# Attention scores in 32-row by 64-column tiles of the TensorE array, in a two-layer transformer kernel

## The chip, the cores and the metric

The kernel runs on one core of a Trainium2 chip. The metric is the device time of one execution in microseconds; a result is the median of several runs. A core has five engines with an instruction stream each: TensorE (PE, matmuls and their weight loads), VectorE (DVE), ScalarE (ACT, activations), GpSimd (POOL) and SyncE (SP, which issues DMAs). An engine takes its instructions in order, and the streams meet at semaphores.

## What is computed

Two layers, each a sliding-window attention and an MLP, on one sequence of 2048 tokens of width 576 (32 heads of 18, window 256, MLP width 4608). Cut to what matters here:

```python
def attention(x):                       # x is layer-normalized
    q, k, v = split(x @ wqkv)           # 32 heads of 18
    scores = einsum("qd,kd->qk", q, k) * 18 ** -0.5
    mask = (q_idx - k_idx >= 0) & (q_idx - k_idx < 256)
    p = softmax(where(mask, scores, -1e9))
    return (p @ v) @ wo

for layer in range(2):                  # the same weights in both
    x = x + attention(layernorm(x))
    x = x + gelu(layernorm(x) @ w1 + b1) @ w2 + b2
```

## The kernel before, in words

**Tiling.** The 2048 tokens are 16 blocks of 128. A chunk `k` is four blocks (512 tokens) of one layer; there are eight chunks, four a layer (`CH`, L455). The 32 heads are eight groups `g` of four heads. The q and k of a group lie transposed in `qT` and `kT`, head `j` of the group in partitions 32j to 32j+31 (18 used, the rest zero), so that the four heads of a group can be four row tiles of the TensorE array, 32 rows by 128 columns each.

**A score unit** (`scores`, L777). Keys of block `so` (counted from the chunk's first block, so -1 and -2 are the blocks before it) are seen by the queries of blocks `so`, `so+1` and `so+2`: the first of these is the diagonal block, the last the far end of the window. The twelve (key block, query block) pairs of a chunk and group are packed into three units of 512 columns by `units_of` (L765). A part of a unit is `(so, qo, nq, col)`: key block, first query block, number of query blocks, first column in PSUM. For each part, and for each of the four heads, one matmul (L789) multiplies the 128 keys (stationary) by up to 384 queries (moving). Scores come out transposed, keys in partitions and queries in columns, one head a PSUM bank: a unit takes four of the eight banks, in two pairs out of 0-1, 2-3, 4-5 (`SC`). In a layer's first chunk the parts with keys before the sequence fall away, and two of its three units shrink to 384 and 256 columns.

ScalarE then takes Exp of two banks at a time into `pT` (L798), GpSimd zeroes what the mask excludes in the diagonal and far blocks (`affine_select`, L819), and TensorE multiplies by v (`pv`, L834) with tiles of 128 rows by 32 columns, four heads beside each other in one PSUM bank (`OUT`). VectorE transposes that bank (L845), divides by the row sums (L848, L851) and transposes again for the output projection (`two_out`, L699, also used for q, k and v).

**MLP.** `G_part` (L899) computes a third of the MLP's first layer for a chunk (the 64 left-over rows at L919 in 64-row tiles, the four full blocks at L931), with Gelu on ScalarE (L934). `mm2` (L946) multiplies by the second weight (L960) into a bank out of `FILL`, and VectorE adds it to the residual (L880). ScalarE loads a table at each change between Exp and Gelu (L973).

**What sets the order.** Nothing runs in the order it is written. Each step is a task with a cost, a latency, a priority and the tiles that it reads and writes; `Plan.schedule` (L257) simulates the five engines, takes the task that can start first (ties by priority), gives PSUM banks out of a list of choices (`Bank`, `place`, L266), adds `SWITCH` (0.095) to TensorE's cost when the tile mode changes (`mode`: "r" scores, "c" P·V, "h" the 64-row tiles, "f" full), and writes the order down as each engine's fixed instruction stream. Score units and MLP groups share a first-in-first-out list ("pa"). `PL.nudge` (L463) adds a number to the priority of every task of a named stage; "ea2" is the first part of the attention of chunk 2, "mb3" the second third of `mm2` of chunk 3, "q5.1" the projections of its second block, and so on.

**Start.** VectorE clears PSUM banks 7 to 4 (L599 to L601, priority -7), then takes the statistics of the first blocks (L620, priority -6), normalizes (L643), and TensorE transposes (L657) into a bank of `FILL`; ScalarE copies out (L660).

Of the kernel before, what the change touches and what calls it, by code (L numbers as in the profile page):

```python
# [421 lines left out]
def build_kernel(nc, A_x, A_wqkv, A_wo, B_x, B_w1, B_b1, B_w2, B_b2, out):  # L422
# [36 lines left out]
    PL = Plan(S, 8)  # L459
# [3 lines left out]
    PL.nudge = {"b": 29.4, "ea0": -2.66, "ld0": 0.01, "ld0+": -29.79, "eb0": 0.53, "ec0": 3.31, "le0+": 114.63, "q1.0": -118.82, "q1.1":  # L463
                -98.11, "q1.2": -0.91, "q1.3": -7.44, "t0": -5.22, "ea1": -89.48, "ga0": -171.5, "ga0+": 5.04, "eb1": -15.16, "ma0": 12.04,
                "ma0+": -17.91, "gb0": -145.98, "ec1": -2.99, "le1+": 16.44, "le1": -20.83, "mb0": -3.03, "q2.1": 45.54, "q2.2": 88.61,
                "q2.3": 55.86, "t1": -120.53, "gc0": -19.84, "gc0+": -25.1, "ln3": 57.08, "mc0": 4.28, "mc0+": 148.11, "ga1": -4.06, "ga1+":
                -6.33, "eb2": -3.01, "ma1": 5.64, "ma1+": 13.09, "gb1": -0.44, "ec2": 3.21, "mb1": 7.94, "mb1+": -24.34, "q3.0": 14.13,
                "q3.1": 131.09, "q3.2": 4.89, "q3.3": 1.84, "t2": -15.58, "gc1": 7.36, "gc1+": -31.57, "mc1": 17.31, "mc1+": -1.81, "ga2":
                -27.48, "ga2+": 158.23, "eb3": 36.01, "ma2": 50.85, "ma2+": 24.11, "gb2": 23.88, "gb2+": 71.77, "ec3": -0.31, "mb2": 60.21,
                "mb2+": -145.98, "q4.0": 0.58, "q4.1": 63.81, "q4.2": 55.53, "t3": 61.03, "gc2": 154.1, "gc2+": 8.93, "ln5": 14.44, "ea4":  # L470
                19.04, "mc2": 63.19, "ga3": 18.64, "ga3+": 0.44, "eb4": 14.59, "ma3": 30.2, "ma3+": 0.16, "gb3": -9.23, "gb3+": -6.16,
                "mb3": 45.14, "q5.0": 113.74, "q5.1": 29.89, "q5.2": -8.93, "q5.3": 76.56, "t4": -2.66, "gc3": 88.61, "gc3+": -48.97, "ln6":
                -15.57, "ea5": -72.82, "mc3": -2.47, "mc3+": 76.5, "ga4+": -33.16, "eb5": 2.91, "ma4": 29, "ma4+": 17.98, "gb4": -4.52,
                "gb4+": -7.43, "mb4": 59.81, "mb4+": -8.12, "q6.0": 1.38, "q6.1": 19.98, "q6.2": -18.44, "q6.3": 63.81, "gc4": 92.87,
                "gc4+": 84.52, "ln7": 31.11, "ea6": -2.66, "mc4": 24.73, "mc4+": 0.51, "ga5": 11.4, "ga5+": 1.49, "eb6": -0.34, "ma5":
                52.45, "ma5+": -6.49, "gb5": -32.33, "gb5+": 51.26, "ec6": -3.2, "mb5": 0.24, "mb5+": -3.62, "q7.0": 24.18, "q7.2": 137.8,
                "q7.3": 1.6, "t6": -24.34, "gc5": 5.59, "gc5+": -171.5, "ea7": 41.87, "mc5": 136.49, "mc5+": -1.6, "ga6": -32.64, "eb7":
                31.31, "ma6": 44.85, "ma6+": -1.66, "gb6": 0.02, "gb6+": -4.59, "ec7": -0.12, "mb6": 104.87, "mb6+": 63.38, "t7": -16.91,
                "gc6+": -0.75, "mc6": -119.39, "mc6+": -8.02, "ga7": -61.44, "ga7+": -11.43, "ma7": -14.13, "ma7+": 9.77, "gb7": 1, "mb7":
                3.96, "mb7+": -8.3, "gc7": 53.28, "mc7": 65.68, "": 0.88}  # L480
# [40 lines left out]
    FILL = (7, 6, 5, 4)  # L521
    OUT = (7, 6, 5, 4)
# [3 lines left out]
    def two(b):  # L526
        return ps[:, b.no * 512:(b.no + 2) * 512].rearrange("p (j c) -> p j c", j=2)
# [71 lines left out]
    for i in OUT:  # L599
        b = Bank((i,))  # L600
        add("dve", lambda e, b=b: e.memset(bank(b), 0.0), writes=[b], cost=0.56, lat=0.1, prio=-7, alloc=[b])  # L601
# [36 lines left out]
    def ln_norm_T(t, i, dst, dname, prio, src=None, srcres=None, dup=False, pe=False):  # L638
# [12 lines left out]
        if pe:  # L651
            b = Bank(FILL)

            def fn(e):
                ins = None
                for c in range(KD):
                    ins = e.transpose(bank(b).bitcast(BF16)[:, c * 128:(c + 1) * 128], xn[:, sl, c * 128:(c + 1) * 128], ident[:, :])  # L657
                return ins
            add("pe", fn, reads=rd + ["ident"], writes=[b], cost=0.5, prio=prio, alloc=[b])
            add("act", lambda e: e.copy(dst[:, :, i * 128:(i + 1) * 128], bank(b).bitcast(BF16)[:, 0:KD * 128].rearrange("p (c q) -> p c q", c=KD)),  # L660
                reads=[b], writes=[f"{dname}{i}"], cost=0.6, lat=0.17, prio=prio)
            return
# [55 lines left out]
    def qkv(k, i, prio0):  # L718
        l, t0, nt = CH[k]
        A = l * NT + t0 + i  # L720
        for n, w in enumerate("qkv"):
# [10 lines left out]
            else:  # L732
# [16 lines left out]
                if k == 0 and (w == "k"):  # L749
                    b = Bank(FILL)  # L750
# [26 lines left out]
    def scores(k, g, parts, prio):  # L777
        l, t0, nt = CH[k]
        T0 = l * NT + t0
        qs, qname = q_of(k)  # L780
# [3 lines left out]

        def fn(e):
            ins = None
            for (so, qo, nq, col) in parts:
                for j in range(4):
                    ins = e.matmul(two(bs[j // 2])[:, j % 2, col:col + nq * 128], k_of(T0 + so)[0][32 * j:32 * j + 32, g, :],  # L789
                                   qs[32 * j:32 * j + 32, g, qo * 128:(qo + nq) * 128], start=True, stop=True, tile_position=(32 * j, 0))  # L790
            return ins
        rd = [f"{qname}{qo + i}" for (so, qo, nq, col) in parts for i in range(nq)] + [k_of(T0 + p[0])[1] for p in parts]
        ncol = sum(p[2] for p in parts) * 128
# [205 lines left out]
    bb = Bank(FILL)  # L999
# [32 lines left out]
    for k in range(NK + 1):  # L1032
        b = 4 * k
# [112 lines left out]
```

## Time and profile before

| | |
|---|---|
| three runs, median (all) | 894.95 us (894.55, 894.95, 897.05) |
| the profiled execution | 897.23 us, of it 895.5 us of span |
| granted TensorE clock, mean | 0.998 |
| score matmuls (L789) | 1408, each with a weight load |
| Exp (L798) | 384, 345.8 us busy |
| masks (L819) | 368, 283.5 us busy |
| P·V matmuls (L834) | 1408 |
| L960, L931, L699 qkv, L919 matmuls, busy | 309.5, 255.0, 136.0, 39.7 us |

The busy rows of a page give the time in which an engine had an instruction in work, the share of the span and the number of instructions. TensorE's matmuls overlap, since one starts while the one before it drains; so the durations of single matmuls don't add up, and the distance from one start to the next is the price. Weight loads (PEld) run beside the matmuls.

### The profile page before, as it was taken

What the parts mean: (1) busy time and instruction counts of PE and PEld (TensorE: products, weight loads), DVE (VectorE), ACT (ScalarE), POOL (GpSimd) and SP (SyncE); (2) the same over time, 40 slices, a digit from 0 to 9 for tenths busy, and PEclk for the clock granted to TensorE, in tenths of its full rate; (3) what the DMA queues carried; (4) which work ended last, traced back from release to release, by engine and by line L of the source; (5) the groups of instructions that cost most, each with busy time, mean ns of one, the idle gap of its engine ahead of it and who ended that gap; (6) DMA issues with size and microseconds to landing.
All of it is one profiled execution on the core that took longest, in us unless ns stands there. A gap on an engine that the chain in (4) does not pass through costs nothing.

```text
span 895.5 us, 19577 instructions
## 1 busy us (share of the span) xinstructions
PE 864.4 (97%) x7849; PEld 506.5 (57%) x7901; DVE 410.1 (46%) x969; ACT 615.8 (69%) x737; POOL 366.2 (41%) x504
## 2 busy tenths in 40 slices
PE   5898999999999999999999999999999999999998
PEld 4555455656566565665655655556556545556665
DVE  6789223863357351763427633375134523161111
ACT  3976888577767788366773868747777689844443
POOL 3677544274244662224431544416444266231100
PEclk9999999999999999999999999999999999999999
DMA  6788537742477333853457342682537632446431
GB/s 177 139 172 173 179 119 182 178 109 81 149 166 158 120 120 98 183 124 121 130 119 181 71 158 86 143 198 67 165 119 147 184 125 71 144 126 176 153 96 50
DMA packets 182649, 122.25 MB, mean 137 GB/s; under 512 B 107424, under 2 KB 181024, under 8 KB 182560
## 3 DMA queue, kind: packets, MB, share of 16 engines
q1 hardware_dynamic: 179152, 115.47, 49.5%
q0 software_dynamic: 1584, 3.54, 1.5%
q10 hardware_dynamic: 1824, 1.99, 0.7%
q8 instruction: 63, 1.03, 0.5%
q14 instruction: 26, 0.21, 0.1%
HBM read 91.28 MB, written 2.36 MB: 105 GB/s over the span
## 4 chain that ended last, share of the span: by engine, by line
PE 54%; DVE 1%; issue 1%; DMA 1%; ACT 1%; POOL 0%
PE ps L960 21%; PE ps L931 18%; PE ps L699 6%; PE ps L789 3%; PE ps L919 3%; PE ps L834 3%; ACT pT L798 1%; DVE x_res L880 0%; DMA xnTa<-xn 0%; DVE st_all L620 0%; DMA xnTm<-xn 0%; DVE xn L643 0%; DVE xn L648 0%; POOL rstd L633 0%; DVE xn L883 0%
## 5 line engine op out<-in xcount | busy, mean ns | idle before, releaser
L819 POOL TENSOR_SCALAR_AFFINE_SELECT pT<-pT 128x512 bf16<-128x512 bf16 (+1 forms) x368 | 283.5, 794 | 266.6 <-ACT pT L798 262.0
L798 ACT ACTIVATE pT<-ps 128x1024 bf16<-128x1024 f32 (+2 forms) x384 | 345.8, 972 | 58.3 <-PE ps L789 57.8
L934 ACT ACTIVATE hT<-ps,b1col 128x512 bf16<-128x512 f32 x288 | 197.8, 687 | 192.8 <-PE ps L931 188.3
L960 PE MATMUL ps<-w_sb,hT 128*128 128x288 bf16 x2304 | 309.5, 287 | 0.2
L960 PEld LDWEIGHTS ps<-w_sb,hT 128*128 128x128 bf16 x2304 | 213.9, 98 | 81.9 <-issue 24.9
L931 PE MATMUL ps<-xnTm,w_sb 128*128 128x512 bf16 x1100 | 255.0, 380 | 4.9 <-issue 3.2
L931 PEld LDWEIGHTS ps<-xnTm,w_sb 128*128 128x128 bf16 x1152 | 109.6, 98 | 137.0 <-issue 19.1
L880 DVE TENSOR_TENSOR x_res<-ps,x_res 128x288 f32<-128x288 f32 x216 | 95.9, 448 | 169.0 <-PE ps L960 158.4
L699 PE MATMUL ps<-wqkv,xnTa 128*128 128x288 bf16 x960 | 136.0, 289 | 3.5 <-DVE qn L742 1.9
L845 DVE STREAM_TRANSPOSE oq<-ps 128x512 f32<-128x512 f32 x64 | 45.8, 715 | 179.0 <-PE ps L834 178.8
L699 PEld LDWEIGHTS ps<-wqkv,xnTa 128*128 128x128 bf16 x960 | 88.4, 98 | 41.4 <-issue 7.8
L742 DVE CAST qn<-ps 128x288 bf16<-128x288 f32 x120 | 53.2, 449 | 35.1 <-PE ps L699 33.0
L942 POOL TENSOR_TENSOR x_res<-x_res,b2bc 128x576 f32<-128x576 f32 x32 | 40.8, 1274 | 69.2 <-ACT hT L934 69.2
L789 PE MATMUL ps<-qT,kT 32*128 32x384 bf16 (+2 forms) x1216 | 64.1, 276 | 2.2 <-ACT pT L798 2.0
L631 POOL TENSOR_SCALAR vtmp<-mv_all 128x1 f32<-128x1 f32 (+1 forms) x43 | 8.5, 197 | 121.4 <-DVE mv_all L622 120.6
L834 PE MATMUL ps<-pT,vA 128*20 128x384 bf16 (+2 forms) x1408 | 50.7, 276 | 2.0 <-ACT pT L798 0.9
L620 DVE BATCH_NORM_STATS2 st_all<-x_res 128x6 f32<-128x288 f32 x104 | 44.8, 448 | 1.2
L919 PE MATMUL ps<-xnTm,w_sb 64*128 64x512 bf16 x288 | 39.7, 381 | 5.5 <-ACT pT L798 3.3
L789 PEld LDWEIGHTS ps<-qT,kT 32*128 32x128 bf16 x1216 | 19.5, 92 | 44.1 <-issue 25.1
L699 PE MATMUL ps<-wo_sb,attT 128*128 128x288 bf16 x320 | 42.8, 286 | 0.1
L834 PEld LDWEIGHTS ps<-pT,vA 128*20 128x20 bf16 x1408 | 25.7, 90 | 26.8 <-issue 13.4
L729 DVE CAST vA<-ps 128x288 bf16<-128x288 f32 x64 | 28.8, 454 | 23.7 <-PE ps L699 23.4
(47 smaller groups left out, 347.6 us busy)
## 6 DMA issues: line engine op xcount, KB each, us to landing
w_sb<-in_B_w_dram SPq DMA_DIRECT2D x48, 864.0 KB, 5.4
w_sb<-in_B_w_dram SPq DMA_DIRECT2D x48, 768.0 KB, 4.7
w_sb<-in_B_w_dram SPq DMA_DIRECT2D x96, 48.0 KB, 4.4
x_res<-in_A_x_dram POOLq DMA_DIRECT2D x3, 1152.0 KB, 7.0
out_dram<-xn SPq DMA_DIRECT2D x16, 144.0 KB, 1.8
wqkv<-in_A_wqkv_dram ACTq DMA_DIRECT2D x3, 576.0 KB, 6.9
w_sb<-in_A_x_dram SPq DMA_DIRECT2D x2, 576.0 KB, 4.2
wo_sb<-in_A_wo_dram SPq DMA_DIRECT2D x4, 144.0 KB, 2.6
```

The source lines that it names most:

```text
L699: ins = e.matmul(bank(bs[o])[:, 0:HB], lhs(c), rhs(c, o * HB), start=(c == 0), stop=(c == KD - 1))
L742: add("dve", lambda e, b=bs[o], dst=dst: e.tensor_copy(dst, heads_of(bank(b))), reads=[bs[o]], writes=[f"qn{sl}h{o}"], cost=0.375, lat=0.1 ...
L789: ins = e.matmul(two(bs[j // 2])[:, j % 2, col:col + nq * 128], k_of(T0 + so)[0][32 * j:32 * j + 32, g, :], qs[32 * j:32 * j + 32, g, qo * ...
L798: add("act", lambda e, h2=h2: e.activation(pT[:, sl, 2 * h2:2 * h2 + 2, lo:hi], two(bs[h2])[:, :, lo:hi], ACT.Exp, scale=SCALE), reads=[bs ...
L819: add("pool", lambda e, ap=ap, pat=pat, sgn=sgn, kind=kind: e.affine_select(ap, ap, pattern=pat, compare_op=(ALU.is_ge if kind == "d" else ...
L834: ins = e.matmul(bank(bo)[32 * j:32 * j + VW, qo * 128:(qo + nq) * 128], vA[:, (T0 + so) % VS, 8 * j + g, :], pT[:, sl, j, col:col + nq * ...
L845: add("dve", lambda e: e.transpose(oq[:, 0:4 * nt, :].rearrange("p b c -> p (b c)"), bank(bo)[:, 0:nt * 128]), reads=[bo, f"aq{(g - 1) % G ...
L880: add("dve", lambda e: e.tensor_tensor(x_res[:, t, sl], bank(b)[:, 0:HB], x_old[:, t, sl], ALU.add), reads=[b] + ([f"xin{t}"] if first els ...
L919: ins = e.matmul(bank(bk)[:, 0:n], w1_sb[64 * b:64 * b + 64, sl, col:col + 128], xnTm[64 * b:64 * b + 64, k % 2, 4, 0:n], start=True, stop ...
L931: ins = e.matmul(bank(bk)[:, 0:n], w1_sb[:, sl, col:col + 128], xnTm[:, k % 2, c, 0:n], start=False, stop=(c == 3))
L934: add("act", lambda e, ff=ff, fl=fl, bk=bk: e.activation(hT[:, fl, 0:n], bank(bk)[:, 0:n], ACT.Gelu_apprx_tanh, bias=b1col[:, ff:ff + 1]), ...
L960: ins = e.matmul(bank(b)[:, 0:HB], hT[:, fl, i * 128:(i + 1) * 128], w2_sb[:, fl, hh * HB:(hh + 1) * HB], start=(fl == 0), stop=(fl == NFH ...
```

## The change

The score matmul of 128 keys is split in two by keys: the lower 64 keys go to the tile at columns 0 to 63 of the array (PSUM partitions 0 to 63), the upper 64 to columns 64 to 127. Each half takes only the queries that some of its keys can see: on the diagonal block the upper half leaves out the first 64 queries, on the far block the lower half leaves out the last 64. So 64 x 64 corners of the PSUM tile are no longer written; Exp still reads them, and the mask zeroes them. All eight banks are therefore cleared at the start, and the steps that put bf16 transposes into PSUM at the beginning (the first normalized blocks, the first k, b1) use banks 7 and 6 alone, which scores never use. `OUT`, the banks of P·V, shrinks to (7, 6) too. The planner's cost of a score unit follows the columns of the larger half. Exp, the masks and P·V are as before. All values of `PL.nudge` are new.

```diff
-    PL.nudge = {"b": 29.4, "ea0": -2.66, "ld0": 0.01, "ld0+": -29.79, "eb0": 0.53, "ec0": 3.31, "le0+": 114.63, "q1.0": -118.82, "q1.1":
...
+    PL.nudge = {"b": -0.69, "ea0": -0.47, "ld0": 1.9, "ld0+": -0.51, "eb0": 38.45, "ec0": -25.47, "le0+": -6.05, "q1.0": -0.95, "q1.1":
...
-    OUT = (7, 6, 5, 4)
+    OUT = (7, 6)
...
-    for i in OUT:
+    for i in range(8):
         b = Bank((i,))
         add("dve", lambda e, b=b: e.memset(bank(b), 0.0), writes=[b], cost=0.56, lat=0.1, prio=-7, alloc=[b])
...
         if pe:
-            b = Bank(FILL)
+            b = Bank((7, 6))
...
                 if k == 0 and (w == "k"):
-                    b = Bank(FILL)
+                    b = Bank((7, 6))
...
+        def seen(part, b):
+
+            so, qo, nq, col = part
+            lo = qo * 128 + (64 * b if qo == so else 0)
+            hi = (qo + nq) * 128 - (64 * (1 - b) if qo + nq - 1 == so + 2 else 0)
+            return lo, hi, col - qo * 128
+
         def fn(e):
             ins = None
-            for (so, qo, nq, col) in parts:
-                for j in range(4):
-                    ins = e.matmul(two(bs[j // 2])[:, j % 2, col:col + nq * 128], k_of(T0 + so)[0][32 * j:32 * j + 32, g, :],
-                                   qs[32 * j:32 * j + 32, g, qo * 128:(qo + nq) * 128], start=True, stop=True, tile_position=(32 * j, 0))
+            for part in parts:
+                for b in range(2):
+                    lo, hi, off = seen(part, b)
+                    for j in range(4):
+                        ins = e.matmul(two(bs[j // 2])[64 * b:64 * b + 64, j % 2, off + lo:off + hi],
+                                       k_of(T0 + part[0])[0][32 * j:32 * j + 32, g, 64 * b:64 * b + 64],
+                                       qs[32 * j:32 * j + 32, g, lo:hi], start=True, stop=True, tile_position=(32 * j, 64 * b))
             return ins
...
-        ncol = sum(p[2] for p in parts) * 128
+        ncol = max(sum(hi - lo for lo, hi, _ in (seen(p, b) for p in parts)) for b in range(2))
         add("pe", fn, reads=rd, writes=bs, cost=0.01 + ncol * 0.00042, prio=prio, lat=0.15, alloc=bs, fifo="pa", mode="r", after=[f"p{sl}h{h}" for h in range(2)] + [f"p{sl}m{m}" for m in range(3)])
...
-    bb = Bank(FILL)
+    bb = Bank((7, 6))
```

## The prediction

> **What bounds the kernel now.** I read the busy rows of the page first, then its slices, then the timeline of TensorE around single score units, then the waits of TensorE, and last the start on VectorE.
>
> ```profile
> span 895.5 us, 19577 instructions
> PE 864.4 (97%) x7849; PEld 506.5 (57%) x7901; DVE 410.1 (46%) x969; ACT 615.8 (69%) x737; POOL 366.2 (41%) x504
> PE   5898999999999999999999999999999999999998
> PEclk9999999999999999999999999999999999999999
> ```
>
> TensorE is busy in 97% of the span, at full granted clock; only some of the first slices are lower. The 31 us in which it is idle are 9.1 us before its first matmul and some 22 us of short waits. So a nanosecond taken off TensorE's stream of instructions counts nearly in full, and so does one put on it. What a score unit costs there is read from the starts in the timeline (start, duration, line, tile; the duration has the pipeline's drain in it, so start to start is what counts):
>
> ```profile
> 312.92 0.83 PE L834 MATMUL ps<-pT,vA 128*20 128x384 bf16 x24
> 313.69 0.40 PE L789 MATMUL ps<-qT,kT 32*128 32x384 bf16 x8
> 314.02 3.85 PE L960 MATMUL ps<-w_sb,hT 128*128 128x288 bf16 x30
> 317.80 0.40 PE L789 MATMUL ps<-qT,kT 32*128 32x384 bf16 x8
> 318.13 1.64 PE L960 MATMUL ps<-w_sb,hT 128*128 128x288 bf16 x12
> 319.71 0.40 PE L789 MATMUL ps<-qT,kT 32*128 32x256 bf16 x8
> ...
> 27.23 0.40 PE L789 MATMUL ps<-qT,kT 32*128 32x384 bf16 x8
> 27.56 1.40 PE L699 MATMUL ps<-wqkv,xnTa 128*128 128x288 bf16 x10
> 28.99 0.29 PE L789 MATMUL ps<-qT,kT 32*128 32x256 bf16 x4
> 29.21 0.30 PE L699 MATMUL ps<-wqkv,xnTa 128*128 128x288 bf16 x1
> ```
>
> A unit of 512 query columns holds TensorE for 0.33 us (317.80 to 318.13), one of 256 columns for 0.22 us (28.99 to 29.21). That is 0.43 ns a column and 0.11 us that do not depend on columns. The four row tiles of a unit run side by side: one after the other, 4 x 512 columns would take 0.88 us. Before a unit there is a fixed price too: 30 matmuls of L960 between two units take 3.78 us and 12 take 1.58 us, so one takes 0.122 us and 0.11 us are left over for each block. The timeline has 192 score units, no two of them in a row, and 64 P·V units; in 51 places a score unit and a P·V unit follow each other directly.
>
> **The change, part by part.**
>
> *Fewer columns.* In each pass over 384 queries the lower and the upper half of the keys get 320 columns each; a lone diagonal or far block has 64 columns in one half and 128 in the other. A full unit so goes from 512 columns to 448 in each half, if the halves run side by side. 64 columns x 0.43 ns = 27.5 ns. This holds for all three units of the 48 (chunk, group) pairs that have keys before them, and for two of the three of the 16 pairs that start a layer (the third, 256 columns, still has 256 in its lower half): 144 + 32 = 176 units x 27.5 ns = -4.8 us.
>
> *Do the halves run side by side?* No row of before has tiles that differ in both row and column. The nearest are P·V's four column tiles, each with a stream of its own out of the same partitions: 24 matmuls of 384, 128 and 256 columns, 4 x 1536 columns in all, take 0.77 us (312.92 to 313.69), 1536 x 0.43 = 0.66 plus 0.11. So four columns of tiles overlap fully, and so do four rows of tiles in the score units. I take it that two by four do as well. The other end: no overlap. Then a full unit streams 896 columns for 512, +165 ns, in 144 + 16 units, and the first-chunk units of 384 and 256 columns become 640 (+110 ns) and 448 (+83 ns), 16 each: 26.4 + 1.8 + 1.3 = +29.5 us.
>
> *More instructions.* 1408 score matmuls (1216 + 128 + 64) become 2816, with as many weight loads; the page should count about 22,400 instructions. In the trace the four matmuls of a pass start 3.5 ns apart. The upper half's four come behind the lower's, so its stream begins 14 ns later. Which half ends last decides: in units that end in 128 far keys' columns (first unit) or in 192 of the upper half (third unit), the upper ends last, and 27.5 - 14 = 13.5 ns are saved; in the second unit the upper half ends in 64 columns and the lower decides, 27.5 ns. A layer's first chunk saves 13.5, 27.5 and 0. Together 48 x 54.5 ns + 16 x 41 ns = 3.3 us instead of 4.8.
>
> *Shorter weight loads.* The loads' rows, mean ns behind the busy time:
>
> ```profile
> L834 PEld LDWEIGHTS ps<-pT,vA 128*20 128x20 bf16 x1408 | 25.7, 90 | 26.8 <-issue 13.4 <-POOL vtmp L631 1.7 <-POOL pT L819 1.5
> L789 PEld LDWEIGHTS ps<-qT,kT 32*128 32x128 bf16 x1216 | 19.5, 92 | 44.1 <-issue 25.1 <-ACT pT L798 13.5 <-ACT hT L934 3.4
> ```
>
> 20 and 128 columns cost 90 and 92 ns, and 64 lie between them: I take no difference. In the trace 384 columns take 173 ns from one pass of a score unit to the next, 13 ns over 384 x 0.417 (0.417 ns being the matmul rows' steady pace, 0.120 us for 288), so some 13 ns of the first load are exposed now; were they to vanish or double and triple, that is -2.5 to +5 us over 192 units.
>
> [...]
>
> *The start.* Eight PSUM banks are cleared on VectorE instead of four.
>
> ```profile
> 2.74 2.11 DVE L601 MEMSET ps<- 128x512 f32 x4
> 4.75 0.76 DVE L620 BATCH_NORM_STATS2 st_all<-w_sb 128x6 f32<-128x288 bf16 x2
> 6.13 0.46 DVE L620 BATCH_NORM_STATS2 st_all<-w_sb 128x6 f32<-128x288 bf16 x1 [0.63 <-DMA w_sb<-in_A_x_dram]
> 8.66 0.41 DVE L643 TENSOR_SCALAR xn<-w_sb,mv_all,rstd 128x576 bf16<-128x576 bf16 x1
> ```
>
> These clearings have priority -7, ahead of the first statistics at -6, and with the same nudge. Four more are 2.0 to 2.1 us. VectorE waited for input for only 0.63 us after that, and that gap is used up (its data land at 6.1 us; VectorE would come at about 7.5). So the first normalized tile comes 1.5 us later, with one more aggregation ahead of it 1.6. TensorE's first matmul waits for just this tile (9.1 us). The transposes of the first chunk also lose two of four banks: a third one then waits for ScalarE's copy, 0.6 us each, but other matmuls can be put in between. I take +1.8 us; the ends are 0 (a pacing by the Exp activations between 25 and 60 us swallows it) and +2.6.
>
> *P·V's output banks.* Two (7, 6) instead of four. In chunks in full course the score units take four of banks 0 to 5, so this asks little; I take 0, and keep the price for the rival.
>
> *The order.* All nudges are replaced, so the whole order of the steps moves. Nothing in before shows the new one. What it can win is bounded by TensorE's waits after the start: 21 of more than 0.25 us add up to 12.4 us (of them 5.6 us between 37 and 93 us, 4.3 us at the changes to Gelu at 728, 761, 789 and 802 us). What it can lose has the same size for want of a nearer row. I take 0, the middle.
>
> Sum: -3.3 (units) + 1.8 (start) = -1.5 us. Against the profiled execution (897.2 us, span 895.5, 1.7 around it) that gives 895.7; against the median of the three runs, 894.95, it gives **893.4**. The profiled one is 2.3 us over the median, and I count from the median.
>
> **The rivals.**
>
> 1. *A better order* (waits gone). For it: a table load at each change from Exp to Gelu leaves holes of 1.52 and 1.22 us on TensorE, and an order can fill them. Against: the sum over all is small. Half of the 12.4 us gone: 893.4 - 6.2 = 887.2.
> 2. *P·V waits for a bank* (slower). Place: the stretches where second-layer MLP matmuls (L960) fill in between the score units. They hold banks 7 and 6 as well, each until VectorE's addition (448 ns at L880) has read it, and P·V can no longer go to 4 or 5. TensorE takes its steps in order, so all behind a waiting P·V waits too, or the planner puts P·V elsewhere and pays one more 0.11 us of fixed price on each side. For it: 64 P·V units, and a bank is held through P·V (0.77) and the transpose that reads it (0.715). Against: now TensorE idles only 2.0 us ahead of P·V in all. At 0.1 us each, 64 give +6.4: 899.8. It decides from about 0.065 us each (4.2 us), where the total passes the 0.3% above.
> 3. *The halves do not overlap.* For it: no row shows such tiles. Against: rows of tiles overlap, columns of tiles overlap. 893.4 + 3.3 + 29.5 = 926.
> 4. *The units gain nothing* (the exposed load doubles, or issue eats it): -1.5 + 3.3 = +1.8, 896.8.
>
> **How the numbers follow.** A measurement of this kernel can tell some 0.3% (2.7 us) from no change: 892.3 to 897.6.
>
> The forecast case with a neutral order has 0.40, and with the open ends of load and start (-2.5 to +5 and -1.8 to +0.8) and a few us of order it reaches from 888 to 899; of it 0.15 is faster, 0.20 the same, 0.05 slower. The better order has 0.24, of it 0.22 faster, 0.02 same. The bank waits, or an order that is worse by as much, have 0.25: slower 0.24, same 0.01. No overlap has 0.04, all slower. No gain in the units has 0.07: 0.05 same, 0.02 slower. That is 0.37 faster, 0.28 same, 0.35 slower. Both signs hold much, so the likeliest case's own range, 888 to 899, stands beside the whole one: 885.5 (rival 1 with a little more than half) to 903 (rival 2 with 0.15 us each).
>
> **What would show it.** Right: in the timeline a score unit of 16 matmuls 32x320 holds TensorE for 0.31 to 0.32 us instead of 0.33; the matmuls' tile reads 32*64; first matmul of TensorE near 10.8 us instead of 9.1; idle ahead of L834 not much over 2 us. Wrong: a unit of 0.45 to 0.5 us (no overlap), 0.34 or more (loads), or idle time of TensorE outside the start that has moved by more than 3 us either way (order, banks); then the order and not the tiles has set the time.

## The result

The changed kernel takes 902.64 us (median of five runs, 900.44 to 904.61) against 895.14 us of the kernel before beside it: a ratio of 1.0081, 95% interval 1.0057 to 1.0104. It is slower, by 0.8%. The time lies in the predicted range of 885.5 to 903 us, at its slow end; the forecast itself was 893.4 us, 0.2% faster.

The profiled execution of the changed kernel took 902.64 us, 5.4 us more than that of before, with a mean granted clock of 0.996. Its page, the lines that answer to those of before:

```profile
span 900.9 us, 22392 instructions
PE 865.3 (96%) x9262; PEld 513.5 (57%) x9313; DVE 412.8 (46%) x973; ACT 615.8 (68%) x737; POOL 367.8 (41%) x504
PE   5888999999999999999999999999999999999998
PEclk9999899999999999999999999999999999999999
```

The 22,400 instructions are there. The slices (22.5 us each) differ in two places alone: TensorE's third has gone from 9 to 8, and the fifth (90 to 112 us) lost some of its granted clock. So I look for the loss before 112 us first. The busy times of that stage, first the kernel before, then the changed one (length, busy PE, PEld, DVE, ACT and POOL with their instructions, then the granted clock, the DMA engines' share and GB/s):

```profile
11.00:105.00 94.00, 86.73 (x890) 51.23 (x894) 66.82 (x161) 70.14 (x94) 55.87 (x76) 1.00 0.74 163
```

```profile
11.00:105.00 94.00, 81.73 (x1044) 50.26 (x1043) 68.91 (x160) 65.25 (x86) 53.85 (x76) 0.96 0.68 136
```

TensorE is busy for 5 us less in 94 us, and ScalarE has 86 instructions in the stretch instead of 94: TensorE waits, and what follows it comes late. VectorE alone is busy for longer.

**Where the time went.** A yardstick for all these kernels is the count of Exp and Gelu activations. The 73rd stands at 100.3 us before and at 108.8 us after, +8.5 us; from there to the end it is 795.2 and 792.1 us, -3.1 us, of which 1.7 is the kernel before's own loss of clock (it ran at half clock from 728.3 to 731.7 us). So the change loses all of its time ahead of that activation.

**A score unit** now, in the timeline of TensorE:

```profile
322.26 0.40 PE L799 MATMUL ps<-qT,kT 32*64 32x320 bf16 x16
322.58 0.83 PE L845 MATMUL ps<-pT,vA 128*20 128x384 bf16 x24
...
328.41 0.40 PE L799 MATMUL ps<-qT,kT 32*64 32x192 bf16 x16
328.74 1.64 PE L971 MATMUL ps<-w_sb,hT 128*128 128x288 bf16 x12
330.31 0.40 PE L799 MATMUL ps<-qT,kT 32*64 32x320 bf16 x16
330.64 1.64 PE L971 MATMUL ps<-w_sb,hT 128*128 128x288 bf16 x12
```

Start to start, a unit costs 0.32 us (322.26 to 322.58) or 0.33 us (328.41 to 328.74, 330.31 to 330.64). Whole tiles cost 0.33. So the eight tiles of a pass do run side by side, and still next to nothing is saved. The weight loads of P·V and of the scores say why only in part:

```profile
L845 PEld LDWEIGHTS ps<-pT,vA 128*20 128x20 bf16 x1408 | 25.9, 91 | 25.5 <-issue 11.0 <-POOL pT L830 2.7 <-POOL vtmp L632 2.1
L799 PEld LDWEIGHTS ps<-qT,kT 32*64 32x64 bf16 x2432 | 25.2, 102 | 43.1 <-issue 29.7 <-ACT pT L809 11.1 <-ACT hT L945 1.3
```

A load of 64 columns has 102 ns where one of 128 had 92, though it loads half as much. What counts is what a pass (the matmuls over one set of queries) costs beyond its streaming. From one pass to the next 320 columns take 160 ns in the trace; at 0.417 ns a column (the slope between rows of 288 columns, 122.5 ns from start to start at L971, and rows of 512, 215.8 ns at L942) they need 133.3, so 26.7 ns come on top, against 13 ns before. I read them as the part of the loads that TensorE waits for. A rival fits the scores as well: a fixed price of 3.3 ns for each matmul of a pass, 13.3 ns for four and 26.7 for eight. P·V speaks against it: its four matmuls also start 3.3 ns apart, but a pass of 384 columns takes 163 to 168 ns from start to start, 3 to 8 over the 160 of its streaming, with loads of only 20 columns. The upper half's first matmul starts 13 ns behind the lower's. A unit that ends with the upper half saves 27.5 ns of columns and pays 13.4 ns more of load and some 13 to 14 ns of issue (the later start of the upper half): nothing is left. One that ends with the lower half keeps 14 ns. Over all 192 units, with waits taken out, the scores held TensorE for 61.2 us before and 60.9 us after.

**The start** on VectorE, and TensorE's first matmul of use:

```profile
2.74 4.27 DVE L602 MEMSET ps<- 128x512 f32 x8
6.92 1.11 DVE L621 BATCH_NORM_STATS2 st_all<-w_sb 128x6 f32<-128x288 bf16 x3
...
9.96 0.41 DVE L644 TENSOR_SCALAR xn<-w_sb,mv_all,rstd 128x576 bf16<-128x576 bf16 x1
```

```profile
10.43 1.25 PE L658 MATMUL ps<-ident,xn 128*128 128x128 bf16 x10 [10.43 <-POOL vtmp L632]
```

The eight clearings take 4.27 us instead of 2.11, the gap in front of the third statistics is gone, and TensorE starts at 10.43 instead of 9.13 us: +1.3. (The view puts this wait down to GpSimd; the first normalized tile, which the matmul reads, was ready at 10.37.)

**The waits of TensorE** between 11 and 105 us, before (waiting line, whom for, us in total, times, longest):

```profile
PE ps L789 <- ACT pT L798: 1.8, 6, 0.7
PE ps L699 <- DVE qn L742: 1.6, 4, 0.7
PE ps L834 <- ACT pT L798: 0.9, 1, 0.9
```

and after:

```profile
PE ps L799 <- ACT pT L809: 3.3, 6, 1.3
PE ps L700 <- DVE qn L743: 3.2, 5, 1.3
PE ps L845 <- DVE qn L743: 1.7, 1, 1.7
```

The same kinds of wait, longer: projections and P·V wait for a bank that VectorE's cast (L743) has still to empty, scores wait for Exp. From the first matmul of use to the first Gelu TensorE idles 7.2 us before and 12.3 us after; from there to the end 11.7 and 9.9. Two of the holes lie close to each other. TensorE's timeline, and VectorE's beside it:

```profile
89.86 0.34 PE L799 MATMUL ps<-x_res 32*64 32x320 bf16 x8 [1.34 <-ACT pT L809]
90.02 0.24 PE L799 MATMUL ps<-x_res,kT 32*64 32x64 bf16 x8
91.95 1.46 PE L845 MATMUL ps<-pT,vA 128*20 128x384 bf16 x24 [1.69 <-DVE qn L743]
93.34 1.38 PE L700 MATMUL ps<-wqkv,xnTa 128*128 128x288 bf16 x5
```

```profile
89.19 0.81 DVE L621 BATCH_NORM_STATS2 st_all<-x_res 128x6 f32<-128x288 f32 x2
89.92 0.90 DVE L644 TENSOR_SCALAR xn<-x_res,mv_all,rstd 128x576 bf16<-128x576 f32 x1
90.75 0.62 DVE L649 TENSOR_SCALAR xn<-x_res,mv_all,rstd 128x64 bf16<-128x64 f32 x1
91.29 0.20 DVE L623 BATCH_NORM_AGGREGATE mv_all<-st_all 128x2 f32<-128x12 f32 x1
91.40 1.13 DVE L743 CAST qn<-ps 128x288 bf16<-128x288 f32 x3
```

P·V waits for the cast at 91.40, and that stands behind statistics and normalizations on VectorE. From 90.8 us, within the second hole, to 97.7 the granted clock is 0.5, and a projection matmul takes 0.24 us from start to start instead of 0.12.

### The profile page after: what moved, and what is told of

Its sections match the earlier page's. It is cut to its first block, busy times and chain, and to the rows that moved or that the text cites. A ratio compares the mean times of both kernels' runs of the same rounds, so it can differ in the third digit from the quotient of the medians.

```text
span 900.9 us, 22392 instructions
## 1 busy us (share of the span) xinstructions
PE 865.3 (96%) x9262; PEld 513.5 (57%) x9313; DVE 412.8 (46%) x973; ACT 615.8 (68%) x737; POOL 367.8 (41%) x504
## 4 chain that ended last, share of the span: by engine, by line
PE 84%; DMA 2%; DVE 1%; issue 1%; ACT 1%; POOL 0%; SPq 0%
PE ps L971 33%; PE ps L942 26%; PE ps L700 11%; PE ps L799 5%; PE ps L845 5%; PE ps L930 4%; DMA xnTa<-xn 1%; ACT pT L809 1%; DMA kT<-qn 0%; DVE x_res L891 0%; DVE xn L644 0%; DVE st_all L621 0%; DVE xn L649 0%; DVE xn L894 0%; DVE oq L856 0%
## 5 line engine op out<-in xcount | busy, mean ns | idle before, releaser
L971 PE MATMUL ps<-w_sb,hT 128*128 128x288 bf16 x2304 | 312.1, 287 | 0.2
L942 PE MATMUL ps<-xnTm,w_sb 128*128 128x512 bf16 x1101 | 254.7, 379 | 4.8 <-issue 3.3
L971 PEld LDWEIGHTS ps<-w_sb,hT 128*128 128x128 bf16 x2304 | 213.0, 98 | 79.9 <-issue 22.9
L942 PEld LDWEIGHTS ps<-xnTm,w_sb 128*128 128x128 bf16 x1152 | 109.2, 98 | 134.2 <-issue 16.7
L743 DVE CAST qn<-ps 128x288 bf16<-128x288 f32 x120 | 53.5, 452 | 49.8 <-PE ps L700 49.5
L799 PE MATMUL ps<-qT,kT 32*64 32x320 bf16 (+4 forms) x2432 | 63.6, 265 | 2.8 <-ACT pT L809 2.6
L799 PEld LDWEIGHTS ps<-qT,kT 32*64 32x64 bf16 x2432 | 25.2, 102 | 43.1 <-issue 29.7
```

The lines of the kernel that those rows point to most:

```text
L743: add("dve", lambda e, b=bs[o], dst=dst: e.tensor_copy(dst, heads_of(bank(b))), reads=[bs[o]], writes=[f"qn{sl}h{o}"], cost=0.375, lat=0.1 ...
L799: ins = e.matmul(two(bs[j // 2])[64 * b:64 * b + 64, j % 2, off + lo:off + hi], k_of(T0 + part[0])[0][32 * j:32 * j + 32, g, 64 * b:64 * b ...
L942: ins = e.matmul(bank(bk)[:, 0:n], w1_sb[:, sl, col:col + 128], xnTm[:, k % 2, c, 0:n], start=False, stop=(c == 3))
L971: ins = e.matmul(bank(b)[:, 0:HB], hT[:, fl, i * 128:(i + 1) * 128], w2_sb[:, fl, hh * HB:(hh + 1) * HB], start=(fl == 0), stop=(fl == NFH ...
```

## The experiments

Two theories at first. **A**: the order, with the banks that go with it. Nudges that suit the planner's figures meet waits on the chip that the planner doesn't know. **B**: the tiles themselves (twice the instructions, the loads). Besides these, **C**, the four added clearings, and **D**, the holes at 88 to 92 us with the clock that is cut behind them.

**Whole tiles in the new order.** The four matmuls of a part are as before; order, clearings and banks as after.

```diff
-            for part in parts:
-                for b in range(2):
...
+            for (so, qo, nq, col) in parts:
+                for j in range(4):
+                    ins = e.matmul(two(bs[j // 2])[:, j % 2, col:col + nq * 128], k_of(T0 + so)[0][32 * j:32 * j + 32, g, :],
+                                   qs[32 * j:32 * j + 32, g, qo * 128:(qo + nq) * 128], start=True, stop=True, tile_position=(32 * j, 0))
```

> The new kernel with its order, banks and clearings kept to the letter (the planner is still told the new cost), but each score matmul again a 32 by 128 tile over all its queries. Theory A (the tiles are worth next to nothing, the time was lost in the order and the banks of the first 110 us): in the trace of the changed kernel a split unit holds TensorE for 0.314 to 0.316 us where it ends in 64 columns and 0.330 where it ends in 128 or 192, against 0.330 for whole units, so 64 units x 14 ns = 0.9 us are given back; about 903.5, ratio to before 1.008 to 1.011. [...]

Measured: 900.62 us, ratio 1.005 [1.0031, 1.0069]; span 898.2 at clock 1.000; TensorE idles 12.3 us up to the first Gelu, the 73rd activation stands at 105.7 us. Most of the loss is there without a single split tile, where a loss that lay in the tiles alone would be gone: B falls as the whole story. The two P·V banks are kept in this run, so it says nothing about them. The size that A gave was too large by 3 us. In the profiles the two differ by 3.1 us at the 73rd activation (105.7 and 108.8). The half clock costs the changed kernel about that much there (half of 6.8 us); and where the changed kernel ran a second time at full clock (below), its 73rd activation stands at 105.8, as with whole tiles. So +8.5 us is 5.4 of start and waits and 3.1 of clock.

**The same with the added clearings cut to one column.**

```diff
-        add("dve", lambda e, b=b: e.memset(bank(b), 0.0), writes=[b], cost=0.56, lat=0.1, prio=-7, alloc=[b])
+        add("dve", lambda e, b=b, w=(512 if i > 3 else 1): e.memset(bank(b)[:, 0:w], 0.0), writes=[b], cost=0.56, lat=0.1, prio=-7, alloc=[b])
```

> As the run before it, and the four added clearings write one column of their bank instead of 512, in the same places of the order. Theory A: VectorE reaches the first statistics some 1.5 to 2 us sooner, TensorE starts at 9.1 to 9.3 us instead of 10.4, and about that much (1.3 us) is gained: 902, ratio about 1.007. Theory C (the clearings at the start are what costs, through everything that follows them on VectorE): 895 to 896, ratio below 1.002.

Measured: 900.27 us, 1.005 [1.0033, 1.0067]. TensorE starts at 8.66 us, yet the first Gelu comes at 100.8 (99.6 in the run above), the idle time is 12.3 us again, and the clock was cut from 88.8 to 95.6. The cut alone costs some 3.4 us here (half of its 6.8), so this profile does not show what became of the earlier start. The executions at full clock do so in part: three of this run have a median span of 897.1 us, four of the run above 897.9, so of 1.8 us at the start some 0.8 came through. C, which needed 895 to 896, falls.

**Eight clearings in the order of before.**

```diff
-    for i in OUT:
+    for i in (7, 6, 5, 4, 0, 1, 2, 3):
         b = Bank((i,))
-        add("dve", lambda e, b=b: e.memset(bank(b), 0.0), writes=[b], cost=0.56, lat=0.1, prio=-7, alloc=[b])
+        add("dve", lambda e, b=b: e.memset(bank(b), 0.0), writes=[b], cost=0.56 if i > 3 else 0.0, lat=0.1 if i > 3 else 0.0, prio=-7, alloc=[b])
```

> The kernel before with its order kept, and four more clearings of banks 0 to 3 on VectorE behind the four that it has (the planner is told that they cost nothing, so that nothing else moves). Theory A: TensorE's first matmul at about 10.5 us instead of 9.1, and the end later by the same 1.3 to 1.6 us, 896.5, ratio 1.001 to 1.002. Theory C: the delay grows along VectorE's queue, 900 or more, ratio 1.005 or more.

Measured: 898.14 us, 1.0017 [1.0005, 1.0029], +1.5 us. TensorE's first matmul of use:

```profile
10.57 1.78 PE L657 MATMUL ps<-ident,xn 128*128 128x128 bf16 x15 [10.57 <-DVE xn L643]
```

At 10.57 instead of 9.13, and every later stage is 1.4 us late, with the waits as before (7.2 and 11.5 us). Here the term of the start is seen by itself: 1.5 us that come through to the end.

**Zero matmuls in the two holes**, so that TensorE is hardly idle from 88 to 92 us.

```diff
+WARM_AT = ((84.70, 20), (86.20, 24))
...
+            ins = e.matmul(bank(4)[:, 384:512], warm[:, 0:128], warm[:, 0:128], start=True, stop=True)
```

> The new kernel with its order kept, and 20 and 24 matmuls of 128 columns on zeros put into the two holes of TensorE at 88.4 to 89.9 and 90.3 to 91.9 us, written to columns of bank 4 that nobody reads. In the changed kernel's trace the granted clock is 0.5 from 90.8 to 97.7 us. Theory D (the clock was cut because TensorE idled there, and the cut costs): granted clock 1.0 throughout, 3 to 4 us less than the changed kernel in the runs that had the cut, median about 899.5, ratio about 1.005. Rival: the holes and not the clock cost the time, so the filling changes nothing, 902 to 903, ratio 1.008.

Measured: 900.95 us, 1.0053 [1.0036, 1.007]. The holes were filled; the rows of two stages (the clock is the third figure from the end):

```profile
46.00:54.00 8.00, 7.18 (x76) 3.24 (x74) 4.92 (x11) 5.49 (x8) 6.41 (x10) 0.57 1.11 209
90.00:98.00 8.00, 7.53 (x141) 5.60 (x141) 8.00 (x18) 5.34 (x6) 6.22 (x10) 1.00 0.38 74
```

From 90 to 98 us the clock is now full (it was 0.57), but in this execution it was cut from 47.0 to 53.8 us instead. Six of the ten executions had a mean clock of 1.000, and so had six of the eleven of the changed kernel without the filling (five for the result, six in the next run). So nothing shows that the filling prevents a cut. D is not settled by this, and the interval overlaps that of the changed kernel.

**The changed kernel once more**, for the share of the clock in its loss.

> The changed kernel once more, beside the other runs of this set. Executions with the same granted clock are to be compared: so far 893 us of span for the kernel before at clock 1.0, 898.7 for the changed one (a single execution), 897.9 with whole tiles in its order. Theory A (the tiles are worth 0.4 to 0.9 us in its favour, the order and the banks of the first 105 us cost 4 us and the clearings 1.3): 897 to 898 us of span at clock 1.0, ratio 1.005 to 1.008, depending on how often the clock is cut. Theory B (split tiles cost time): 899 or more at clock 1.0, so over a microsecond more than with whole tiles.

Measured: 901.33 us, 1.0064 [1.0045, 1.0084]; in the profiled execution the clock was 1.000 and the span 900.3, 4.8 us over that of before, which had lost 1.7 us to its own cut. At full clock throughout, the median span is 899.0 us in five executions, against 893.4 in six of before beside them: +5.6 us. The cut is not needed for the loss. The two holes need not bring a cut either; here they are again, and the clock stays full (the third figure from the end of the last line):

```profile
89.24 0.34 PE L799 MATMUL ps<-x_res 32*64 32x320 bf16 x8 [1.34 <-ACT pT L809]
91.33 0.83 PE L845 MATMUL ps<-pT,vA 128*20 128x384 bf16 x24 [1.69 <-DVE qn L743]
90.00:98.00 8.00, 6.21 (x93) 4.05 (x95) 7.74 (x20) 5.83 (x7) 5.24 (x8) 1.00 0.71 121
```

Theory A's span of 897 to 898 is missed by 1 us, and theory B's "899 or more" is just met. Over before, it is 5.6 us with split tiles here and 4.9 with whole ones (897.9 against 893.0, on another chip): up to some 0.7 us may lie in the tiles in this order.

**Corrected price, other nudges.** The planner gives a unit 27 ns for its 64 columns, the chip 0 to 14. The cost was corrected and new nudges were found for it.

```diff
-        ncol = max(sum(hi - lo for lo, hi, _ in (seen(p, b) for p in parts)) for b in range(2))
+        tot = [sum(hi - lo for lo, hi, _ in (seen(p, b) for p in parts)) for b in range(2)]
+        ncol = sum(p[2] for p in parts) * 128 - (32 if tot[0] != tot[1] else 0)
```

> The changed kernel with the same tiles, banks and clearings, but the planner's price of a score unit set to what the trace shows (512 columns' worth, 32 fewer where the halves differ, in place of 448), and the nudges searched anew for that, by the end that the planner computes. That end is 888.0 us by its own count; the kernel before has 889.5 by that count and took 5 to 6 us more on the chip, the changed one 887.1 and took 14 more. Theory A (the order cost the time): 893 to 896, ratio 0.997 to 1.002, holes of TensorE over 0.25 us before 105 us that add up to 7 us or less instead of 11. Theory F (two banks for P.V and eight clearings make any order late): 900 or more, ratio above 1.004.

Measured: 903.77 us, 1.009 [1.0073, 1.0106], span 901.3 at clock 1.000. A's figure (893 to 896) failed: an honest price for the unit doesn't help. It looked like theory **F**, that two P·V banks and the added clearings make any order late.

**The longer half first**, in that order, so that the shorter one ends with it.

```diff
-                for b in range(2):
+                for b in ((1, 0) if tot[1] > tot[0] else (0, 1)):
```

> As the run before it, with the longer half of the keys first where the halves differ. In units that end in 128 columns of the upper half (far block), the upper half now starts first and 14 ns fall away: 48 units x 14 ns = 0.7 us less than that run, and those units at 0.316 us instead of 0.330 in the timeline. If not the issue of four matmuls but the load decides, the unit stays at 0.330 and the time the same.

Measured: 905.33 us, 1.01 [1.0082, 1.0117]. The unit does get shorter:

```profile
323.63 0.38 PE L802 MATMUL ps<-qT,kT 32*64 32x320 bf16 x16
323.95 1.64 PE L974 MATMUL ps<-w_sb,hT 128*128 128x288 bf16 x12
```

The units that end in the far block go from 330 to 317 ns, and the scores from 60.7 to 60.0 us in all; TensorE's idle time after the start rises from 24.8 to 26.1 us. In these two profiles what is saved on TensorE turns into waiting, and the time does not fall.

**Late clearings and another order.** Banks 0 to 3 are cleared behind the first normalized blocks, with new nudges (longer half first and corrected price stay).

```diff
-    for i in range(8):
+    for i in (7, 6, 5, 4):
...
+    for i in (0, 1, 2, 3):
+        b = Bank((i,))
+        add("dve", lambda e, b=b: e.memset(bank(b), 0.0), reads=["rstd3"], writes=[b], cost=0.56, lat=0.1, prio=-5.5, alloc=[b])
```

> Tiles and banks of the changed kernel, longer half first; the clearings of banks 0 to 3 moved behind the normalization of the first four blocks (banks 4 to 7 are cleared first, as before), the price of a unit as in the trace, and the nudges searched anew; the planner's end is 884.0. Theory A: TensorE starts at 9.1 us, and with the same 5 to 6 us over the plan it takes 889 to 891, ratio 0.993 to 0.996, faster than both kernels. Theory F: 897 or more.

Measured: 902.34 us, 1.0071 [1.0052, 1.0089], although TensorE starts at 8.96 us; A had 889 to 891, and F's "897 or more" is met again. The order has a hole of 3.96 us that ends at 80.66, ahead of scores that wait for the transpose of `kT`, and the clock is cut twice (52 to 56 and 79.5 to 86.4 us).

**The old kernel in new orders.** If F holds, whole tiles with four P·V banks must do well in a new order too. The rival is theory **G**: an order that the planner has just liked best meets waits that the planner doesn't know, whatever the banks. Three sets of nudges for the kernel before, nothing else changed: one found from those of after, one found from zero, and its own with a few refined.

> The kernel before (whole tiles, four clearings, four banks for P.V) with nudges searched anew from the changed kernel's; planner's end 892.1 us. The two new orders for the changed kernel's tiles and banks ran 13 to 17 us over the planner's end, and 5 to 12 of these come before the first Gelu at about 105 us; the kernel before runs 6 over, 2.5 of them there. Theory G (an order that a planner has just liked best meets waits on the chip that it doesn't know, whatever the banks; the old order happens to be free of them): 5 us or more late by the first Gelu, 902 to 908 in all, ratio 1.007 or more. Theory F (two banks for P.V and more clearings make an order late): 2 to 3 us late by the first Gelu, 897 to 899, ratio 1.002 to 1.005.

Measured: 907.76 us, 1.0141 [1.0122, 1.0159].

> The kernel before with nudges searched anew from all zeros; planner's end 889.2 us, as good as that of the old order (889.5). Theory G: 5 us or more late against the plan by the first Gelu, 899 to 905, ratio 1.004 or more. Theory F: 2 to 3 us late there, 894 to 896, ratio 0.998 to 1.002.

Measured: 901.41 us, 1.0063 [1.0043, 1.0083].

> The kernel before with its own nudges refined by the same search; planner's end 888.2 us, 1.3 less than the old order. If the planner's count can be trusted near an order that runs well: 893.8, ratio 0.9985. Theory G says that a change of a few nudges is enough to meet a new wait: 896 or more, ratio above 1.001.

Measured: 901.35 us, 1.0068 [1.0053, 1.0083]. So F isn't needed: with no split tile, no bank taken away and no clearing added, a new order costs 6 to 12 us. The last of the three shows one such loss in the open, since the two streams of TensorE are alike up to 74.2 us. Ten matmuls of the output projection (from 72.9 us) end there in both, and then come scores, before and in the refined order:

```profile
74.19 0.40 PE L789 MATMUL ps<-x_res,kT 32*128 32x256 bf16 x8
```

```profile
77.87 0.40 PE L791 MATMUL ps<-x_res,kT 32*128 32x256 bf16 x8 [3.61 <-DMA kT<-qn]
```

They wait 3.61 us for the transpose of `kT`. SP's queue shows why, before and in the refined order (start, length of the issue):

```profile
66.31 1.79 SPq L561 DMA_DIRECT2D w_sb<-in_B_w_dram  x3
68.41 1.30 SPq L761 DMA_TRANSPOSE kT<-qn  x1
```

```profile
66.31 1.79 SPq L563 DMA_DIRECT2D w_sb<-in_B_w_dram  x3
68.21 1.25 SPq L763 DMA_TRANSPOSE qT<-qn  x1
69.56 2.98 SPq L763 DMA_TRANSPOSE kT<-qn  x1
```

`qT` and `kT` have changed places. The transpose of `kT` is issued 1.15 us later and lands 4.1 us later: it takes 8.2 us from issue to landing (69.56 to 77.73) instead of 5.25. In this window the shortest of these transposes lands in 3.1 us; a weight load of 768 KB and a load of `x_res` of 1152 KB are on their way beside the slow one. That these slow it is argued from the order of the issues, not shown by itself. A step that looks free in the plan moved a transfer behind other transfers.

**A third order for the changed kernel**: late clearings, longer half first, corrected price, nudges found from zero. F and G forecast the same here, a late order.

> As the run with late clearings, with nudges searched from all zeros; planner's end 886.4 us. Theory F: 5 us or more late against the plan by the first Gelu, as the other two orders with these banks, and 899 to 904, ratio 1.004 or more. Theory G says the same; the two differ in the runs of the kernel before. An order that runs as planned would give 892.

Measured: 896.82 us, 1.0014 [1.0004, 1.0024]; span 895.5 at clock 1.000. Split tiles, two P·V banks and eight clearings run within 0.15% of the kernel before, so they do not make every order late: F falls. G's figure (899 or more) fails as well: a new order can lose 6 to 12 us, as the three runs above show, but need not. TensorE's holes of over 0.25 us up to the first Gelu add up to 6.1 us (5.6 before, 10.5 in the changed kernel).

**What the tiles are worth, at one order.** The third order again, and the same order with whole tiles (the edit of the first experiment), run on the same chip.

> The run with late clearings and the third order once more, beside the next two, which keep its order: 896 to 898, ratio about 1.0014.

> The same order, banks and clearings, but 32 by 128 tiles again for every score matmul. In the split kernel's trace a unit with unequal halves (longer half first) holds TensorE 14 ns less than a whole one, 48 + 48 + 32 of them, one with equal halves the same, and one of 256 columns 13 ns more: 128 x 14 ns less 16 x 13 = 1.6 us for the split. Theory A (the tiles are worth what the unit shows): 1.6 us slower than the run beside it, ratio about 1.003. Theory W (what TensorE gains it waits away): no difference beyond 0.5 us. Theory B (split tiles cost time): faster than the run beside it.

Measured: 896.23 us, 1.0012 [0.9997, 1.0027], with split tiles; 896.49 us, 1.0008 [0.9996, 1.0019], with whole ones. In the pages, split and then whole:

```profile
span 894.2 us, 22457 instructions
PE 868.1 (97%) x9317; PEld 511.9 (57%) x9317; DVE 416.0 (47%) x973; ACT 615.1 (69%) x737; POOL 367.0 (41%) x504
```

```profile
span 894.3 us, 19641 instructions
PE 869.2 (97%) x7909; PEld 504.9 (56%) x7909; DVE 415.7 (46%) x973; ACT 615.8 (69%) x737; POOL 368.0 (41%) x504
```

2816 more instructions with split tiles (22457 to 19641), 1.1 us less of busy TensorE, and spans that are 0.1 us apart. The split tiles take 60.4 us of TensorE from start to start, the whole ones 61.5; TensorE idles 14.3 us after the start with the split ones, 12.9 with the whole ones. In these two executions the 1.1 us are there and all of it is waited away. The times cannot tell 1.1 us from nothing: the medians are 0.3 us apart, and each interval is 1 us or more wide to either side. They do exclude that split tiles cost the 5 us that the changed kernel lost.

**Opening the clock early.** The third order with the clearings and 16 zero matmuls on TensorE ahead of the first use, and the order of before with its four clearings and 24 zero matmuls there (the last line below is that of the second). In the kernel before, projection matmuls of 288 columns start 0.240 us apart up to 14.84 us and 0.1225 us apart from 14.98 us on, and the records of its granted clock begin at 14.87 us with 1.0; in the changed kernel the same step comes at 15.7 us.

```diff
+    def clear(e, i):
+        for c in (0, 256):
+            ins = e.matmul(bank(i)[:, c:c + 256], warm[:, 0:128], warm[:, :], start=True, stop=True)
+        return ins
...
+    PL.first = [(4.9, lambda e: warm_fn(e, 0, 24))]
```

> The same order with split tiles; all eight banks are cleared by matmuls on zeros on the idle TensorE (the four late clearings on VectorE write one column), and 16 more such matmuls of 256 columns follow. In all traces the granted clock is full only from about 14 us, while TensorE starts at 8.6 to 10.4 and has hardly a gap until 22. Theory: with the clock opened before the first real matmul, up to half of the 5 to 6 us until 14 us are gained, and VectorE is free of the clearings; 893 to 895.5, ratio 0.997 to 1.000. Rival: what is bound there is the input (weights land at 8.8 to 10.8 us), so at most 0.5 us are gained.

Measured: 900.57 us, 1.0055 [1.0036, 1.0074]. The theory had 893 to 895.5. The first real matmul is at 9.13 us (8.67 in the run of the third order above); a new hole of 2.30 us ends at 75.26, the clock is cut from 76.5 to 79.9, and the first Gelu comes at 98.7 instead of 95.5 us.

> The kernel before with its order and whole tiles; its four clearings are done by matmuls on zeros on the idle TensorE, and 24 more of 256 columns follow, before the first real matmul at 9.1 us. Theory: clock full by 9 us instead of 14.9, 1.5 to 3 us gained, 892.5 to 894, ratio 0.997 to 0.9985. Rival: bound by the weights' landing, at most 0.5 us.

Measured: 898.7 us, 1.0035 [1.0021, 1.005]; the theory had 892.5 to 894. TensorE's start:

```profile
2.79 4.16 PE L617 MATMUL ps<-warm 128*128 128x256 bf16 x24
9.08 1.78 PE L668 MATMUL ps<-ident,xn 128*128 128x128 bf16 x15 [2.13 <-DVE xn L654]
```

The clock was full from 5.6 to 9.0 us and 0.5 from 9.0 to 12.4, just when the real work came after 2.13 us of idling. The start itself stays at 9.08, since VectorE, free of the clearings, waits 0.86 and 1.54 us for its input. Up to the 48th activation 0.5 us were won, later more was lost. No kernel here beats the one before.

## Why the prediction was wrong

- *Fewer columns, halves side by side*: right. 320 columns in both halves, eight tiles at once; the rival with units of 0.45 to 0.5 us did not come.
- *More instructions*: right, 13 to 14 ns ahead of the upper half.
- *Shorter weight loads, "I take no difference"*: wrong, and within the bounds that stood beside it. What a pass costs beyond its streaming doubled, from 13 to 26.7 ns. With it the units gave -0.3 us instead of -3.3: for the units, the rival in which they gain nothing came true. The mean durations, 90 and 92 ns, to which I went by nearness, don't show what is exposed: they would have it that 20 and 128 columns cost the same, where P·V's passes have 3 to 8 ns on top and the scores' 13. (At the pace of 0.417 ns a column 288 columns do not take 0.120 us, as I had it: these rows take 0.1225 us and those of 512 columns 0.2158, and 0.417 is the slope between them.) Why a load of 64 columns leaves twice as much on top as one of 128, no run shows; that it is the load at all is my reading.
- *The start*: right, +1.3 us in the profile and +1.5 in the run that had only the clearings, for a forecast of 1.8.
- *P·V's two banks*: one hole of 1.7 us that ends at 91.95 is of that rival's kind (a bank held until VectorE gets to it), but at a projection's cast and not behind L960. In all TensorE idles 2.6 us ahead of P·V, against 2.0 before; the rival needed some 4 us more. The third order runs with two banks within 0.15%, and the old kernel with four loses as much in new orders. So two banks are neither enough for the loss nor needed for it; the order of the changed kernel was not run with four.
- *The order, "I take 0, the middle"*: this step failed, and it is the largest miss. TensorE's idle time ahead of the first Gelu went from 7.2 to 12.3 us, and in the profiled execution a clock cut of 3.1 us came on top. At full clock the change costs 5.6 us; less the start (+1.3) and the units (-0.3) some 4.6 us are left for the order, banks included. The prediction's own sign of this came: idle time outside the start moved by more than 3 us, from 18.9 to 22.2 us, and to 24.2 in the second execution. The bounds of ±12.4 us were wide enough; the middle was not the likeliest value. That the whole range held the time is luck: its end of 903 us was worked out for waits of 0.15 us ahead of each P·V, 9.6 us together, and those grew by 0.6 us in all. Of seven new orders run here (after, three more for split tiles, three for whole ones) none was faster, and the ratios go from 1.0012 to 1.0141.
- *Two readings of the waits*: of the 22 us of "short waits" 3.1 us lie behind the last matmul. And the hole of 1.52 us that was put down to a table load ends with an Exp at 727.84, before that load starts at 728.63.

The planner's own end does not rank the orders:

| kernel | tiles | planner's end, us | time on the chip, us | ratio |
|---|---|---|---|---|
| late clearings, other order | split | 884.0 | 902.34 | 1.0071 |
| late clearings, third order | split | 886.4 | 896.82 | 1.0014 |
| after | split | 887.1 | 902.64 | 1.0081 |
| corrected price | split | 888.0 | 903.77 | 1.009 |
| before, refined | whole | 888.2 | 901.35 | 1.0068 |
| new order 2 | whole | 889.2 | 901.41 | 1.0063 |
| before | whole | 889.5 | 895 to 896 | 1 |
| new order 1 | whole | 892.1 | 907.76 | 1.0141 |

The plan of before says 889.5 and it runs in 895; a plan that is 5 us shorter runs in 902. (The plan of after still has the too low price of a score unit; the other split ones have the corrected price.) The lag of the profiled span behind the plan goes from 6 us (before) over 9 (third order) and 14 (after) to 17 (late clearings, other order), and part of it is there by the 72nd activation, shortly behind the first Gelu: 2.5 us for before, 4.0 for the third order, 8.2 for after, 3 of these for the cut clock.

**What stays open.** Which steps of a plan become waits is shown for single holes only: a transpose behind another in SP's queue, a cast behind layer norm on VectorE. What cuts the clock, and when, is not settled: the same holes came with a cut in one execution of the changed kernel and without one in another. And since the kernel with whole tiles in the new order (1.005) and the changed one (1.0064 and 1.0081) have intervals that overlap, up to some 0.3% may lie in the tiles in that order; in the third order no difference is seen. How the order of before was found is not on record, so neither is why it has fewer waits than the seven.

## What to carry to other kernels

A change that comes with a new order is two changes. Replay the same order with the old instructions before crediting or blaming the new ones; and where the order comes from a planner that has not been checked against runs, don't count a new one as a coin toss around zero: the seven orders here lost 0.1 to 1.4%. Splitting the tiles to leave out columns saved their streaming here, an estimated 27.5 ns a unit, less 13.4 ns read as the load and 14 ns for the issue of the added matmuls. And of the 1.1 us that the split took off the busiest engine in the third order nothing was won, since its idle time went from 12.9 to 14.3 us; look at an engine's idle time after a change as well as at its busy time.

## What the runs showed of the hardware

- Tiles of 32 rows by 64 columns, four by two, run all at once: the eight matmuls of a pass, 320 columns each, take 160 ns together, and the upper half starts 13 ns behind the lower.
- A pass of score matmuls costs more beyond its streaming (0.417 ns a column) with weights of 64 columns in column tiles (26.7 ns) than with 128 columns without them (13 ns); P·V's of 384 queries, with weights of 20 columns in column tiles, 3 to 8 ns. That it is the exposed part of the weight load is inferred from these three.
- The DMA transposes into `kT` land in 3.3 us in the median; one took 5.25 us with weight loads issued just ahead of it, and 8.2 us one place further back in the queue.
- The granted clock fell to 0.5 for 3.4 or 6.8 us at a time, and the size of a hole did not decide it: holes of 1.34 and 1.69 us came with 6.8 us of it in one execution and with none in another of the same kernel, one of 2.13 us with 3.4 us, and one of 3.61 us (the refined order) with none: the seven projection matmuls right behind its scores take 1.03 us.
